# A sparse-attention and Fourier-mixing kernel: block sums and a mask moved to GpSimd, row statistics split between VectorE and ScalarE, one weight tile converted later

## The chip, the cores and the metric

The kernel runs on one core of a Trainium2 chip, in float32. The metric is the device time of one execution in microseconds. Engines are written as in the profile: PE (TensorE), DVE (VectorE), ACT (ScalarE), POOL (GpSimd), SP (SyncE, which here issues most of the transfers).

## The reference, cut to what matters

Four batches, eight heads, 768 tokens, 64 elements per head. Each token attends to its neighbours within 16 places and to one summary per block of 32 tokens (the maximum of the keys, the mean of the values). The result goes through a real Fourier mix over tokens and channels, a layer norm and a two-layer MLP.

```python
k_sum = k.reshape(B, H, nb, block, D).max(axis=3)
v_sum = v.reshape(B, H, nb, block, D).mean(axis=3)
...
a = softmax(concat([where(|i - j| < window, q k^T, -1e9), q k_sum^T + log(block)]))
attn_out = a @ concat([v, v_sum])
...
mixed = real(fft(fft(x, axis=1), axis=2))
u = x + mixed
mu = mean(u);  var = mean((u - mu) ** 2)
un = (u - mu) / sqrt(var + 1e-06)
return u + relu(un @ w_ch1) @ w_ch2
```

`w_ch1` (512 x 2048) and `w_ch2` (2048 x 512) arrive as 64-bit floats, which the kernel turns into 32-bit ones itself.

## The kernel before, in words

The program is one long sequence for the four batches, written with generators that are interleaved, so that the attention of batch b + 1 runs beside the MLP of batch b. Both MLP products are done by a Strassen-Winograd scheme with seven products instead of eight; its sums of operands and of results are additions on DVE, POOL and ACT, and its matmuls are the lines L1381 (hidden layer: hx, hy, hz), L1651 (o) and L1674 (ox, oy, oz).

**Batch 0's attention** (`first_attention`) goes head pair by head pair; its order on PE and DVE is written out by hand. Query and key tiles are transposed on PE (qk), scores (sc) go through an exponential on ACT into p, which DVE masks; p times values gives av, which DVE scales by the reciprocal of its last column into x. The summary values need sums over blocks of 32 rows: `add_blocks(gg)` (L606) halves a 96 x 2048 tile by five additions (1024, 512, 256, 128, 64 columns) into vbs, for heads 0 to 3 (gg = 0) and 4 to 7 (gg = 1); a matmul (vs, L767) spreads these.

**Batch 0's Fourier mix and norm** (`gen_fourier(0)`): after the folded token transform (t, f, y), the channel transform mx (L1297, L1299) is added to x on DVE for each of six tiles of 128 tokens, in two halves of three tiles. `bn_stats` and `bn_aggr` (L1306, L1307) give mean and variance of each row. For each half a chain of small operations on 128 x 3 elements (L1319 to L1331: sign, epsilon, a bit trick for the reciprocal root and three Newton steps) gives the factors; two tiles are then normalised on DVE (L1279) and one on ACT (L1276), into big. PE transposes big (unt, L1353), the copies (L1354) make u, and `_right_sums` makes the three Strassen sums of u on DVE (128 x 1536, 768, 768).

**Batch 1's attention** (`gen_attention(1)`) runs beside that: for each pair g of heads qk(1,g), sc(1,g), ss(1,g) (scores of the summaries, L811), av(1,g) (L829, L834), vs(1,g) (L817). ACT copies the qk tiles out of PSUM (L729, into kt and qt) and takes the exponentials (L800, L812). `add_later_blocks(1, gg)` (L642) makes batch 1's block sums from four 96 x 512 pieces: three additions and a `tensor_reduce` (L650) on DVE for batch 1, six additions on POOL for later batches. Tiles of batch 1's p are masked by `near` (L1048): for g = 0 on POOL, for g = 1 on DVE. All attention tiles share four PSUM banks (tag "attn"); the dense work has the other four.

**Weights** (`gen_weights`, plan at L1064): each tile of w_ch1 or w_ch2 is loaded as raw words (`load_raw`, issued by SP), converted by `exponents` and `convert` (in turn DVE L1096, ACT L1097, DVE L1109, ACT L1110, DVE L1112, DVE L1114 and a DVE multiplication), and for w_ch1 three Strassen sums follow. The finished tile is also stored to memory for the later batches (dw). An entry of the plan waits until the program has reached its stage: (1, 1), the second tile of w_ch1, waits for ("mx", 0).

**What sets the order.** The scheduler places instructions from the order of the program's text, with priorities. `tc.issue_after(marks[...])` keeps an instruction behind a marked one: the transposes of batch 0's first half stand behind the scores sc(1,0), those of the second half behind av(1,0) (L1347). On every engine instructions then run in the order of the program; SP's transfers too are issued in order.

Of the kernel before, what the change touches and what calls it, by code (L numbers as in the profile page):

```python
# [16 lines left out]
P = 128  # L17
# [471 lines left out]
def _main_program(ctx, tc, q, k, v, moe_w_ch1, moe_w_ch2, out):  # L489
# [116 lines left out]
    def add_blocks(gg):  # L606
        raw, vb = to_add[gg]
        n = BLOCK * D // 2
        while n > D:
            tt(raw[:, 0:n], raw[:, 0:n], raw[:, n:2 * n], ADD)  # L610
            n //= 2
        tt(vb, raw[:, 0:D], raw[:, D:2 * D], ADD)
# [29 lines left out]
    def add_later_blocks(b, gg):  # L642
        f = BLOCK // 4
        raw, vb = to_add[b, gg]
        add = gtt if b > 1 else tt
        add(raw[0], raw[0], raw[1], ADD)
        add(raw[2], raw[2], raw[3], ADD)
        add(raw[0], raw[0], raw[2], ADD)
        if b == 1:
            nc.vector.tensor_reduce(out=vb, in_=raw[0].rearrange("p (f d) -> p d f", d=D), op=ADD, axis=AX.X)  # L650
            return
        while f > 2:
            f //= 2
            gtt(raw[0][:, 0:f * D], raw[0][:, 0:f * D], raw[0][:, f * D:2 * f * D], ADD)
        gtt(vb, raw[0][:, 0:D], raw[0][:, D:2 * D], ADD)
# [149 lines left out]
    def sum_scores(b, g, p):  # L805
        km, qt = km_bufs[g % 2], nat[b, g]
        ps = abank([P, S2], f"ss_{b}_{g}")
        for h in range(2):
            for e in range(2):
                rows, r = slice(D * e, D * (e + 1)), 64 * (e ^ h) + 32 * h  # L810
                nc.tensor.matmul(ps[r:r + 32, :], km[rows, :], qt[rows, S2 * h:S2 * (h + 1)], start=True, stop=True)  # L811
        nc.scalar.activation(out=p, in_=ps, func=AF.Exp, scale=SC)  # L812
# [178 lines left out]
    def gen_attention(b):  # L991
# [13 lines left out]
        for g in range(NP + 1):  # L1005
# [42 lines left out]
            if b == 1 and g < 2:  # L1048
                for h in range(2):
                    with tc.issue_after(marks["u"]) if g else ExitStack():  # L1050
                        (tt if g else gtt)(held[0][:, h], held[0][:, h], near[:, h], ALU.mult)
# [93 lines left out]
    def gen_weights():  # L1145
        for f, j, stage in plan:
# [3 lines left out]
            while True:  # L1150

                with tc.issue_after(marks[stage]) if stage in marks else ExitStack():
                    done = next(steps, steps) is steps
                if done:
                    break
                yield
        for to, wv in stores:
# [66 lines left out]
    def gen_fourier(b):  # L1224
# [56 lines left out]
        for half in range(2):  # L1281
# [3 lines left out]
            if b == 0:  # L1285
                both = spool.tile([P, HT, 2], FP, tag="both", bufs=2, name=f"both_{half}")
            for i in range(HT):
# [4 lines left out]
                else:  # L1292
# [10 lines left out]
                    with tc.issue_after(marks["un", 0]) if t > HT else ExitStack():  # L1303
                        tt(xv, ps, xv, ADD)
                    bst = spool.tile([P, 6], FP, tag="bst", name=f"bst_{b}_{t}")
                    nc.vector.bn_stats(out=bst, in_=x[:, t, :])  # L1306
                    nc.vector.bn_aggr(out=both[:, i], in_=bst)  # L1307
# [23 lines left out]
            ins = nc.vector.tensor_tensor(out=z, in0=minus, in1=y, op=ALU.mult)  # L1331
            if b == 0:
# [9 lines left out]
        for t in range(NST):  # L1342
# [4 lines left out]
            with tc.issue_after(marks[("av", 1, 0) if half else ("sc", 1, 0)]) if b == 0 else ExitStack():  # L1347
# [10 lines left out]
            yield  # L1358
        _right_sums(tt, u.rearrange("p a k n -> p a (k n)"))
# [517 lines left out]
```

## Time and profile before

| | us |
|---|---|
| time of the kernel, median of 3 runs | 789.2 (786.87 to 791.82) |
| span of the profiled execution | 787.6 |
| PE busy | 771.0 (98%) |
| DVE busy | 536.3 (68%) |
| ACT busy | 241.8 (31%) |
| POOL busy | 74.6 (9%) |

The profiled execution is another than the three timed ones: its own time is known only as its span, from the first to the last instruction. The change touches the stretch from 25 to about 135 us. A row of the timeline has the start, the duration, the engine and line, the operation, what it writes and reads, how many instructions the row holds, and in brackets the idle time before it and what ended that. A row of the windows has the busy time of each engine in a stretch, the number of instructions in it, the mean granted TensorE clock and the share of DMA time. A row of the groups has busy time and the mean of one instruction in ns.

### The profile page before, as it was taken

The numbers are of one execution on the slowest core, as the hardware profiler recorded it, in microseconds if no ns is written. First come the engines' busy times: TensorE is split into PE (matmuls) and PEld (weight loads), VectorE is DVE, ScalarE is ACT, GpSimd is POOL, SyncE is SP. The second block draws the span as 40 slices with busy tenths as digits, with TensorE's granted clock in tenths as the row PEclk, the third lists the DMA queues.
The fourth block names the chain that finished last, engine by engine and source line by source line (L and its number), as shares of the span: only waits on it lengthen the run. The fifth ranks groups of instructions, "written<-read, shape, count | busy, mean of one in ns | idle before, by whom it ended". The sixth has DMA issues, their size and how long they took to land.

```text
span 787.6 us, 14943 instructions
## 1 busy us (share of the span) xinstructions
PE 771.0 (98%) x6076; PEld 582.2 (74%) x6076; DVE 536.3 (68%) x1121; ACT 241.8 (31%) x561; POOL 74.6 (9%) x99
## 2 busy tenths in 40 slices
PE   8999899999999999999999999999999999999997
PEld 5878455445579866688569876688659889889986
DVE  4899979697988647652577635463476987766762
ACT  3555557236535112100226112210126214204300
POOL 0000000000000020200120011300030004201500
PEclk9999999999999999999999999999999999999999
DMA  8999785796966369996344159830614044204001
GB/s 182 200 279 236 178 281 158 232 251 230 222 196 177 71 174 189 261 156 143 123 185 141 54 172 180 210 109 10 253 48 158 27 164 170 94 1 188 1 28 57
DMA packets 133933, 121.87 MB, mean 155 GB/s; under 512 B 94528, under 2 KB 115232, under 8 KB 133664
## 3 DMA queue, kind: packets, MB, share of 16 engines
q1 hardware_dynamic: 132736, 118.53, 54.8%
q0 software_dynamic: 576, 2.10, 0.7%
q8 instruction: 50, 0.82, 0.5%
q10 hardware_dynamic: 544, 0.20, 0.1%
q14 instruction: 27, 0.22, 0.1%
HBM read 97.22 MB, written 23.59 MB: 153 GB/s over the span
## 4 chain that ended last, share of the span: by engine, by line
PE 86%; DVE 7%; ACT 3%; DMA 2%; issue 1%; SPq 0%; DVEq 0%
PE ox L1674 18%; PE hx L1381 15%; PE oz L1674 9%; PE hz L1381 7%; PE oy L1674 4%; PE t L1554 4%; PE o L1651 4%; PE hy L1381 4%; PE y L1258 3%; PE f L1554 2%; PE mx L1217 2%; PE sc L793 2%; PE av L829 2%; DMA words<-in_v_dram 1%; PE av L834 1%; PE ss L811 1%
## 5 line engine op out<-in xcount | busy, mean ns | idle before, releaser
L1381 PE MATMUL hx<-u,w 128*128 128x384 f32 x384 | 140.4, 494 | 1.3 <-ACT h L1398 0.8
L1381 PEld LDWEIGHTS hx<-u,w 128*128 128x128 f32 x384 | 70.9, 190 | 53.5 <-ACT p L800 3.7
L1674 PE MATMUL oz<-w,s 128*128 128x256 f32 x336 | 81.7, 380 | 0.0
L1674 PE MATMUL ox<-w,s 128*128 128x256 f32 x336 | 80.1, 380 | 0.0
L1674 PE MATMUL ox<-w,h 128*128 128x256 f32 x336 | 79.6, 381 | 0.0
L1674 PEld LDWEIGHTS ox<-w,h 128*128 128x128 f32 x336 | 63.0, 190 | 10.7 <-issue 1.2
L571 DVE TENSOR_TENSOR x<-ox,x 128x256 f32<-128x256 f32 x84 | 35.5, 423 | 51.2 <-PE ox L1674 50.8
L1381 PE MATMUL hz<-u,w 128*128 128x384 f32 x192 | 70.3, 487 | 0.0
L1674 PEld LDWEIGHTS ox<-w,s 128*128 128x128 f32 x336 | 63.0, 190 | 9.3 <-DVE s L571 0.4
L1674 PEld LDWEIGHTS oz<-w,s 128*128 128x128 f32 x336 | 63.3, 190 | 8.9 <-DVE x L571 0.4
L1381 PEld LDWEIGHTS hz<-u,w 128*128 128x128 f32 x192 | 36.3, 190 | 25.0
L1392 ACT COPY h<-hx 128x384 f32<-128x384 f32 x24 | 11.5, 479 | 119.6 <-PE hx L1381 119.6
L1651 PE MATMUL o<-w,h 128*128 128x512 f32 x96 | 42.3, 595 | 0.7 <-DVE w L571 0.7
L1674 PE MATMUL oy<-w,h 128*128 128x256 f32 x168 | 40.7, 381 | 0.7 <-ACT h L1603 0.7
L1557 ACT COPY f<-t 128x192 f32<-128x192 f32 x52 | 15.8, 303 | 78.3 <-PE t L1554 78.1
L1533 POOL TENSOR_SCALAR h<-h 128x768 f32<-128x768 f32 x12 | 25.4, 2127 | 137.5 <-DVE h L1513 137.5
L574 POOL TENSOR_TENSOR vb<-vb 96x512 f32<-96x512 f32 (+2 forms) x20 | 20.9, 1050 | 182.4 <-DMA vb<-in_v_dram 116.2
L571 DVE TENSOR_TENSOR x<-oz,x 128x256 f32<-128x256 f32 x42 | 17.8, 423 | 26.7 <-PE oz L1674 26.4
L1674 PEld LDWEIGHTS oy<-w,h 128*128 128x128 f32 x168 | 31.5, 190 | 5.9 <-ACT h L1603 1.5
L1381 PE MATMUL hy<-u,w 128*128 128x384 f32 x96 | 35.2, 488 | 0.0
L1651 PEld LDWEIGHTS o<-w,h 128*128 128x128 f32 x96 | 18.0, 190 | 22.7 <-issue 20.7
L571 DVE TENSOR_TENSOR h<-hy,h 128x384 f32<-128x384 f32 x24 | 13.4, 556 | 26.3 <-PE hy L1381 26.1
(222 smaller groups left out, 1328.8 us busy)
## 6 DMA issues: line engine op xcount, KB each, us to landing
w<-dw SPq DMA_DIRECT2D x42, 896.0 KB, 5.9
words<-in_moe_w_ch_dram SPq DMA_DIRECT2D x32, 512.0 KB, 5.9
dw<-w SPq DMA_DIRECT2D x12, 896.0 KB, 7.6
vw<-in_v_dram SPq DMA_DIRECT2D x47, 192.0 KB, 6.2
out_dram<-x SPq DMA_DIRECT2D x23, 256.0 KB, 2.0
vb<-in_v_dram SPq DMA_DIRECT2D x24, 192.0 KB, 7.2
kn<-in_k_dram SPq DMA_DIRECT2D x9, 384.0 KB, 6.2
qn<-in_q_dram SPq DMA_DIRECT2D x9, 384.0 KB, 7.3
```

Source lines behind the costliest of these rows:

```text
L571: return nc.vector.tensor_tensor(out=out, in0=in0, in1=in1, op=op).ins
L574: return nc.gpsimd.tensor_tensor(out=out, in0=in0, in1=in1, op=op).ins
L793: ins = nc.tensor.matmul(ps[h][r:r + 64, i, :], kt[rows, o:o + 64], qt[rows, o:o + BLOCK], start=True, stop=True)
L829: nc.tensor.matmul(av[r][32 * j:32 * (j + 1), t, :], p[rows, h, i - NB2 * h, :], vw[rows, i, :], start=(t == 0), stop=False, skip_group_ch ...
L1217: nc.tensor.matmul(out, y[:, g], table, start=False, stop=True, skip_group_check=True)
L1258: nc.tensor.matmul(y, fgs[b][par][:, st, P * g:P * (g + 1)], fs[par][:, g % 2, st, :], start=(st == 0), stop=(st == n - 1))
L1381: ins = nc.tensor.matmul(ps, w[:, a, kk, :], u[:, r, kk, :], start=start and kk == 0, stop=stop and kk == 1, skip_group_check=True)
L1533: nc.gpsimd.tensor_scalar(out=t, in0=t, scalar1=0.0, scalar2=None, op0=ALU.max)
L1554: marks["two"] = nc.tensor.matmul(o, left(j, a, m), rhs(r, m), start=m in (1, 5), stop=m in (2, 3, 4, 5, 7), skip_group_check=True).ins
L1557: nc.scalar.copy(out={1: f[:, 0], 6: f[:, 1], 7: g}[m], in_=t)
L1651: nc.tensor.matmul(ps, h[:, n, hf, P * t:P * (t + 1)], wt[2, b, j][:, 2 * hf:2 * hf + 2, :], start=(n, hf) == (0, 0), stop=(n, hf) == (NC ...
L1674: nc.tensor.matmul(ps, left[a][:, n, :], wt[2, b, j][:, r, :], start=start and n == 0, stop=stop and n == NC - 1, skip_group_check=True)
```

## The change

Six things are done. (1) `add_blocks(1)`, the second set of batch 0's block sums, goes from DVE to POOL. (2) Batch 1's two sets of block sums go from DVE to POOL; the reduction becomes three smaller additions. (3) The mask of batch 1's pair g = 1 goes from DVE to POOL. (4) Batch 0's statistics: the addition of mx to x becomes a `scalar_tensor_tensor` that also gives the row sum; ACT squares (sum - 512 x) with a row sum of its own, so `bn_stats` and `bn_aggr` fall away, and with them one small operation per half; the scale 1/512^3 and the sign move into two of the small operations. (5) The transposes of batch 0's second half stand behind ss(1,0) and no longer behind av(1,0). (6) The second entry of the weight plan waits, after its first step, until the transposes of u have been written into the program.

```diff
     def add_blocks(gg):
...
+        add = gtt if gg else tt
         while n > D:
-            tt(raw[:, 0:n], raw[:, 0:n], raw[:, n:2 * n], ADD)
+            add(raw[:, 0:n], raw[:, 0:n], raw[:, n:2 * n], ADD)
             n //= 2
-        tt(vb, raw[:, 0:D], raw[:, D:2 * D], ADD)
+        add(vb, raw[:, 0:D], raw[:, D:2 * D], ADD)
...
     def add_later_blocks(b, gg):
-        add = gtt if b > 1 else tt
-        add(raw[0], raw[0], raw[1], ADD)
-        add(raw[2], raw[2], raw[3], ADD)
-        add(raw[0], raw[0], raw[2], ADD)
-        if b == 1:
-            nc.vector.tensor_reduce(out=vb, in_=raw[0].rearrange("p (f d) -> p d f", d=D), op=ADD, axis=AX.X)
-            return
+        gtt(raw[0], raw[0], raw[1], ADD)
+        gtt(raw[2], raw[2], raw[3], ADD)
+        gtt(raw[0], raw[0], raw[2], ADD)
         while f > 2:
...
     def sum_scores(b, g, p):
+        marks["ss", b, g] = ins.ins
...
     def gen_attention(b):
-                        (tt if g else gtt)(held[0][:, h], held[0][:, h], near[:, h], ALU.mult)
+                        gtt(held[0][:, h], held[0][:, h], near[:, h], ALU.mult)
...
     def gen_weights():
                 yield
+                if (f, j) == (1, 1) and stage != ("u", 0):
+                    stage = ("u", 0)
+                    while stage not in issued:
+                        yield
...
     def gen_fourier(b):
-                        tt(xv, ps, xv, ADD)
-                    bst = spool.tile([P, 6], FP, tag="bst", name=f"bst_{b}_{t}")
-                    nc.vector.bn_stats(out=bst, in_=x[:, t, :])
-                    nc.vector.bn_aggr(out=both[:, i], in_=bst)
+                        nc.vector.scalar_tensor_tensor(out=xv, in0=ps, scalar=1.0, in1=xv, op0=ALU.mult, op1=ADD,
+                                                       accum_out=minus[:, i:i + 1])
+                    nc.scalar.activation(out=un[:, t, :], in_=x[:, t, :], func=AF.Square, bias=minus[:, i:i + 1],
+                                         scale=-float(DM), accum_out=var[:, i:i + 1])
...
-            if b == 0:
-                nc.vector.tensor_scalar(out=minus, in0=both[:, :, 0], scalar1=-1.0, scalar2=None, op0=ALU.mult)
-                nc.vector.tensor_scalar(out=var, in0=both[:, :, 1], scalar1=1e-6, scalar2=None, op0=ADD)
-            else:
-                nc.vector.tensor_scalar(out=var, in0=var, scalar1=1.0 / DM, scalar2=1e-6, op0=ALU.mult, op1=ADD)
+            nc.vector.tensor_scalar(out=var, in0=var, scalar1=1.0 / DM ** (1 if b else 3), scalar2=1e-6, op0=ALU.mult, op1=ADD)
...
-            ins = nc.vector.tensor_tensor(out=z, in0=minus, in1=y, op=ALU.mult)
-            if b == 0:
+            if b:
+                tt(z, minus, y, ALU.mult)
+            else:
+                ins = nc.vector.scalar_tensor_tensor(out=z, in0=minus, scalar=-1.0 / DM, in1=y, op0=ALU.mult, op1=ALU.mult)
                 marks["mx", 0] = ins.ins
...
-            with tc.issue_after(marks[("av", 1, 0) if half else ("sc", 1, 0)]) if b == 0 else ExitStack():
+            with tc.issue_after(marks[("ss", 1, 0) if half else ("sc", 1, 0)]) if b == 0 else ExitStack():
...
+        if b == 0:
+            marks["u", 0] = marks["u"]
+        issued.add(("u", b))
         _right_sums(tt, u.rearrange("p a k n -> p a (k n)"))
```

The orders below show two places. In a name such as hx_3_1505 the first number is the tile and the last one an instance; lines are those of each kernel's own text, so the same statement may stand at L811 before and at L808 now.

The first place is PE where batch 0's second half is transposed. Before, the transposes unt_3 to unt_5 stand behind the last matmuls of av(1,0), directly ahead of ss(1,1):

```order
L834 MATMUL av_0_1_1086<-vs,p_0_954 128x2x65
L1353 MATMUL unt_3_1147<-ident,big_734 128x128 x4
L1353 MATMUL unt_4_1170<-ident,big_734 128x128 x4
L1353 MATMUL unt_5_1183<-ident,big_734 128x128 x4
L811 MATMUL ss_1_1160<-qt_1_831,km_83 32x384 x4
L726 MATMUL qk_2_0_1195<-ident,kn_2_725 128x128 x3
```

In the change they stand inside the scores sc(1,1) (the rows of unt_4 and unt_5 alternate four times):

```order
L790 MATMUL sc_1_1_1006<-qt_1_826,kt_81 64x32 x2
L790 MATMUL sc_1_0_1005<-qt_1_826,kt_81 64x32
L1351 MATMUL unt_3_1118<-ident,big_736 128x128 x4
L1351 MATMUL unt_4_1134<-ident,big_736 128x128
L1351 MATMUL unt_5_1140<-ident,big_736 128x128
```

So 12 transposes have moved ahead of 35 of the 48 pairs of score matmuls and of all of av(1,0).

The second place is ACT where batch 1's pair g = 3 is copied out of PSUM (kt_81 and qt_3 from qk_3). Before, the four copies of kt stand together behind the exponential of ss(1,2), and a weight conversion (words, w_0_1) stands ahead of the copies of qt:

```order
L812 ACTIVATE p_2_1466<-ss_2_1471 128x384
L729 COPY kt_81<-qk_3_0_1539 64x384 x2
L729 COPY kt_81<-qk_3_1_1545 64x384 x2
L1392 COPY h_0_1244<-hx_3_1505 128x384
L1389 ACTIVATE h_0_1244<-h_0_1244 128x384
L1398 COPY h_0_1244<-hx_3_1505 128x384
L1389 ACTIVATE h_0_1244<-h_0_1244 128x384 x2
L1411 ACTIVATE h_0_1244<-hx_2_1390 128x384
L1097 ACTIVATE words<-words,rebias 128x1024
L1110 ACTIVATE w_0_1_1366<-w_0_1_1366 128x1024
L1400 COPY h_0_1244<-hz_3_1507 128x384
L729 COPY qt_3_1538<-qk_3_0_1551 64x384 x2
```

In the change:

```order
L810 ACTIVATE p_2_1438<-ss_2_1443 128x384
L726 COPY kt_81<-qk_3_0_1511 64x384 x2
L726 COPY kt_81<-qk_3_1_1517 64x384
L1095 ACTIVATE words<-words,rebias 128x1024
L1108 ACTIVATE w_0_3_1346<-w_0_3_1346 128x1024
L1390 ACTIVATE h_0_1202<-h_0_1202 128x384
L1412 ACTIVATE h_0_1202<-hx_2_1363 128x384
L1390 ACTIVATE h_0_1202<-h_0_1202 128x384
L726 COPY kt_81<-qk_3_1_1517 64x384
L726 COPY qt_3_1510<-qk_3_0_1523 64x384 x2
L726 COPY qt_3_1510<-qk_3_1_1529 64x384 x2
L817 ACTIVATE vs<-vs_2_1536,half 128x64 x2
```

So the conversion of the fourth tile of w_ch1 (w_0_3) and three activations of the hidden layer now stand between the third and the fourth copy of kt.

The third place is PE after ss(1,2) in the change, where the transposes of qk(1,3), vs and av(1,2) come close together:

```order
L808 MATMUL ss_2_1443<-qt_2_1148,km_82 32x384 x4
L1382 MATMUL hx_2_1363<-u_802,w_0_2_1226 128x384 x2
L1382 MATMUL hz_2_1365<-u_802,w_0_2_1226 128x384 x2
L723 MATMUL qk_3_0_1511<-ident,kn_3_988 128x128 x3
L723 MATMUL qk_3_1_1517<-ident,kn_3_988 128x128 x3
L723 MATMUL qk_3_0_1523<-ident,qn_3_990 128x128 x3
L723 MATMUL qk_3_1_1529<-ident,qn_3_990 128x128 x3
L815 MATMUL vs_2_1536<-vbs_1_1185,sel 128x64
L1382 MATMUL hx_2_1363<-u_802,w_0_2_1226 128x384 x2
L827 MATMUL av_2_0_1587<-vw_84,p_2_1438 32x65 x17
```

Before, hidden-layer products of two tiles and six products of o (L1651) lay between the first of these transposes and av(1,2); now two matmuls of hx lie between vs(1,2) and it.

More of the change, by code (lines that the diff above doesn't have):

```diff
@@ L810, in sum_scores @@
                 rows, r = slice(D * e, D * (e + 1)), 64 * (e ^ h) + 32 * h
-                nc.tensor.matmul(ps[r:r + 32, :], km[rows, :], qt[rows, S2 * h:S2 * (h + 1)], start=True, stop=True)
+                ins = nc.tensor.matmul(ps[r:r + 32, :], km[rows, :], qt[rows, S2 * h:S2 * (h + 1)], start=True, stop=True)
+        marks["ss", b, g] = ins.ins
         nc.scalar.activation(out=p, in_=ps, func=AF.Exp, scale=SC)
@@ L1284, in gen_fourier @@
             minus, var = stat[:, 0], stat[:, 1]
-            if b == 0:
-                both = spool.tile([P, HT, 2], FP, tag="both", bufs=2, name=f"both_{half}")
             for i in range(HT):
@@ L1330, in gen_fourier @@
                 nc.vector.scalar_tensor_tensor(out=y, in0=z, scalar=1.5, in1=y, op0=ADD, op1=ALU.mult)
-            ins = nc.vector.tensor_tensor(out=z, in0=minus, in1=y, op=ALU.mult)
-            if b == 0:
+            if b:
+                tt(z, minus, y, ALU.mult)
+            else:
+                ins = nc.vector.scalar_tensor_tensor(out=z, in0=minus, scalar=-1.0 / DM, in1=y, op0=ALU.mult, op1=ALU.mult)
                 marks["mx", 0] = ins.ins
```

## The prediction

> **What bounds the kernel now.** I read the page first, then the list of what PE waits for, then the windows, then the timeline and the transfers where the waits lie.
>
> ```profile
> PE 771.0 (98%) x6076; PEld 582.2 (74%) x6076; DVE 536.3 (68%) x1121; ACT 241.8 (31%) x561; POOL 74.6 (9%) x99
> PE 86%; DVE 7%; ACT 3%; DMA 2%; issue 1%; SPq 0%; DVEq 0%
> ```
>
> PE is busy for 771.0 of 787.6 us. So all of its idle time is 16.6 us, and the change removes no matmul: work taken off DVE is worth only what PE waits for DVE. That list is short (line of the waiting matmul, what it waited for, us in total, times, longest):
>
> ```profile
> PE ss L811 <- issue: 2.5, 1, 2.5
> ...
> PE o L1651 <- DVE w L571: 0.7, 1, 0.7
> ...
> PE av L777 <- DVE p L571: 0.6, 1, 0.6
> ...
> PE ss L811 <- DVE km L700: 0.3, 1, 0.3
> ```
>
> The windows place it (busy us of each engine, then the granted clock and the DMA share):
>
> ```profile
> 60.00:80.00 20.00, 19.58 (x387) 16.80 (x386) 18.61 (x60) 10.71 (x22) 1.97 (x2) 1.00 1.19 243
> 80.00:100.00 20.00, 16.84 (x160) 9.15 (x158) 18.42 (x26) 11.09 (x21) 0.00 (x0) 0.91 0.70 162
> ...
> 120.00:140.00 20.00, 20.00 (x63) 10.92 (x62) 18.35 (x26) 12.43 (x24) 0.00 (x0) 1.00 0.70 178
> ```
>
> From 60 to 80 us DVE is the fuller helper (18.61 of 20), and the chain of work that ended last runs through its x, bst, norm and big lines there. Yet PE lost only 0.42 us in that window, since scores and av filled the time. From 120 to 140 us PE loses nothing at all. The one large loss is at 81 us, and it is no wait for DVE:
>
> ```profile
> 80.80 0.48 PE L811 MATMUL ss<-qt,km 64*32 64x384 f32 x1 [0.32 <-DVE km L700]
> 83.81 1.50 PE L811 MATMUL ss<-qt,km 64*32 64x384 f32 x7 [2.54 <-issue]
> ```
>
> PE stops in the middle of eight like matmuls. The transfers in these microseconds show why:
>
> ```profile
> DMA  9999999999999989777676655933221211100000
> ...
> q8 instruction: 1, 0.02, 3.7%
> ```
>
> This is 80 to 82 us: the data queue is full until 81.2, and the only instruction packet of the window (0.02 MB) starts when it drains. In the window from 76 to 80 us there is none, though the data queue runs at full share. I read it so: PE's next instructions queue behind the transfer issued last, qn at 75.52.
>
> ```profile
> 75.52 0.94 SPq L551 DMA_DIRECT2D qn<-in_q_dram  x1
> ```
>
> After the stop the granted clock is half for one stretch:
>
> ```profile
> 81.27:83.81 2.54, 0.00 (x1) 0.00 (x0) 2.54 (x4) 0.52 (x2) 0.00 (x0) 1.00 0.06 15
> 83.85:87.26 3.41, 3.41 (x13) 1.45 (x13) 3.41 (x5) 1.50 (x3) 0.00 (x0) 0.50 0.94 265
> ```
>
> 3.41 us at 0.50 cost up to 1.7 us more, so the stop is worth 2.54 + 1.7 = 4.2 us. [...]
>
> **The change part by part.**
>
> *Batch 0's second block sums to POOL.* DVE is freed of four additions, 2.72 us, and a small one:
>
> ```profile
> 29.38 2.72 DVE L571 TENSOR_TENSOR words<-words 96x1024 f32<-96x1024 f32 x4
> ```
>
> and the matmul that reads the sums stands at
>
> ```profile
> 34.11 0.63 PE L767 MATMUL vs<-vbs,sel 96*32 96x64 f32 x8
> ```
>
> The words are issued at 17.89 us and land 8.7 us later, at 26.6:
>
> ```profile
> L551 SPq DMA_DIRECT2D words<-in_v_dram x1: 493/493/493, 17.9 to 17.9; - x1
> ...
> DMA to landing us min/median/max: 8.7/8.7/8.7
> ```
>
> POOL's prices for such additions:
>
> ```profile
> L574 POOL TENSOR_TENSOR vb<-vb 96x512 f32<-96x512 f32 x12 | 15.8, 1324 | 181.8 <-DMA vb<-in_v_dram 116.2 <-ACT p L800 65.3
> ...
> L574 POOL TENSOR_TENSOR vb<-vb 96x256 f32<-96x256 f32 x4 | 2.9, 722 | 0.3
> ...
> L574 POOL TENSOR_TENSOR vb<-vb 96x128 f32<-96x128 f32 x4 | 2.2, 554 | 0.3
> ...
> L574 POOL TENSOR_TENSOR p<-p,near 128x384 f32<-128x384 f32 x2 | 2.0, 1006 | 28.6 <-ACT p L800 28.6
> ...
> L574 POOL TENSOR_TENSOR vbs<-vb 96x64 f32<-96x64 f32 x4 | 1.3, 315 | 0.3
> ```
>
> The 1024 columns are not shown; twice 1.32 is 2.65. The sum is 2.65 + 1.32 + 0.72 + 0.55 + 0.32 = 5.6 us, done at 32.2, 1.9 us ahead of the matmul that reads them. Cost 0; the cover is gone if the words land 1.9 us later. The gain is at most the 0.6 us that av L777 waited for p behind DVE's queue at 42 us.
>
> *Batch 1's block sums and the mask.* The reductions and the matmuls that read all such sums (duration least, median, most; first and last start):
>
> ```profile
> L817 PE MATMUL vs<-vbs,sel x24: 221/273/323, 74.3 to 520.6; 96*128 96x64 f32 x24
> ...
> L650 DVE TENSOR_REDUCE vbs<-vb x2: 1021/1022/1022, 61.2 to 123.5; 96x64 f32<-96x512 f32 x2
> ```
>
> DVE saves 1.02 us and three additions, about 0.68 each (what bst below takes over 512 columns), so 3.06 us twice, and two masks of some 0.55. POOL needs 3 x 1.32 + 0.72 + 0.55 + 0.32 = 5.6 us a set and 2.0 us for the masks. The first reduction ended at 62.2 and its matmul came at 74.3; the second at 124.5 and 130.04 (row below). 2.5 us more than now leaves over 9 us and 3 us. Cost 0.
>
> *Statistics.* What goes from DVE:
>
> ```profile
> L1306 DVE BATCH_NORM_STATS2 bst<-x 128x6 f32<-128x512 f32 x6 | 3.9, 679 | 0.0
> L1307 DVE BATCH_NORM_AGGREGATE both<-bst 128x2 f32<-128x6 f32 x6 | 1.0, 170 | 0.0
> ```
>
> That is 6 x 0.68 + 6 x 0.17: 5.1 us, and a small operation in each half. ACT gains six Squares, by the like operation of later batches 0.72 us each, 4.3 us, into the window where it was busy for 10.7 of 20:
>
> ```profile
> L1313 ACT ACTIVATE big<-x,stat 128x512 f32<-128x512 f32 x6 | 4.3, 717 | 0.1
> ```
>
> The addition with a row sum is not shown: from 0.68 us, as bst over the same 512 columns, to twice that if the sum takes a pass of its own, 4.1 us over six tiles. I take the first; at the other end the 3.5 us just below are gone and with them the gain.
>
> In the chain of the second half the last Square (0.72 and two handovers) stands where two bst and their aggregates stood (1.4 with overlap): little is gained there. But the half starts some 3.5 us sooner (one reduction, three bst, the aggregates). DVE was through with normalising when it took up the next weight tile, at 78.50; now that is near 75. PE begins the scores sc(1,1) at 74.66:
>
> ```profile
> 78.50 0.69 DVE L1096 TENSOR_SCALAR words<-words 128x1024 int32<-128x1024 int32 x1
> 74.66 1.58 PE L793 MATMUL sc<-qt,kt 64*64 64x32 f32 x91
> ```
>
> The transposes, moved ahead of 35 pairs of these scores, are reached by PE at about 75 too. Little or no wait: 0, at worst 1 us, and that would be spent ahead of the stop at 81 us.
>
> Together these three parts relieve PE of the waits for DVE in the list: the 0.3 at 80.80, perhaps the 0.6 of av. I take **-0.5** (from -0.9 to 0).
>
> *The stop at 81 us.* PE's matmuls up to it are the same ones in another order, so its instructions run out at the same count. kn and qn are issued by SP as before. PE reaches that count at best 0.3 us sooner and waits for the same transfer: I take **0**, with -4.2 as the other end if the order of the transfers has shifted enough. What is earlier in u is worth nothing then, as hidden products begin after the stop.
>
> *The later second weight tile.* DVE began its conversion at 78.50; now the transposes of u are written ahead of most of it. This pushes the conversions of the second, third and fourth tile back. Where it lands is ACT's queue at the copies of qk(1,3): between the third and fourth copy of kt stand a conversion and three activations. Their prices:
>
> ```profile
> L1097 ACT ACTIVATE words<-words,rebias 128x1024 int32<-128x1024 int32 x7 | 8.0, 1149 | 5.0 <-DVE words L1096 4.8
> L729 ACT COPY qt<-qk 64x384 f32<-64x384 f32 x13 | 6.7, 513 | 0.2
> L1110 ACT ACTIVATE w<-w 128x1024 f32<-128x1024 int32 x6 | 6.3, 1044 | 0.0
> ...
> L1389 ACT ACTIVATE h<-h 128x384 f32<-128x384 f32 x12 | 6.1, 522 | 5.4 <-DVE h L571 5.4
> ```
>
> av(1,2) needs two of the four attention banks, which these copies free. From the third copy of kt to the second copy of qt ACT has 0.51 + 1.15 + 1.04 + 3 x 0.52 + 0.51 + 2 x 0.51 = 5.8 us. PE has, in that time, about nine transposes, vs and two hx:
>
> ```profile
> 129.38 0.82 PE L726 MATMUL qk<-ident,qn 128*128 128x128 f32 x6
> 130.04 0.33 PE L817 MATMUL vs<-vbs,sel 96*128 96x64 f32 x2
> ```
>
> that is 1.2 + 0.3 + 0.8 = 2.3 us. So PE waits up to 3.5 us; nothing if ACT has run ahead by then. Before, some twenty dense products lay there and PE lost nothing. I take **+2.0**, nearer the full wait, since the orders of both engines show no other work in between. On PE all of the hidden layer is queued behind av(1,2), so this wait reaches the end undiminished. The 0.7 us that o waited for a converted w I count as gone, **-0.4** (from -0.7 to 0), because conversions of w_ch2 now have less in front of them on a lighter DVE.
>
> Sum: -0.5 + 0 + 2.0 - 0.4 = **+1.1**, a span of 788.7 against 787.6. The median of the runs is 1.6 above that profiled span, so the time is 790.3 us.
>
> **The rivals.**
>
> *The stop vanishes.* If in the new order the packet of instructions comes ahead of qn's transfer, 4.2 us fall away: 787.6 - 4.2 + 1.1 = 784.5, as a time 786.1; with no wait at av(1,2), 784. For it: the gap is a coincidence of a full queue and a count of instructions. Against: both stay where they were.
>
> *Slower: the wait at av(1,2) halves the clock.* The mechanism is ACT's queue: the copy that frees a bank stands behind a conversion, and the conversion behind DVE (idle of 4.8 us behind L1096 in the row above). From about 2.5 us of idleness the trace shows the clock halved for 3.41 us, 1.7 us more. With the full 3.5 us: 787.6 - 0.5 + 3.5 + 1.7 = 792.3, as a time 793.9, and up to 797 if the late tiles make hx wait as well. For it: DVE is at 18.35 of 20 in that window already. Against: DVE loses some 11 us of work ahead of it.
>
> *POOL holds up DVE.* POOL gets 18.8 us of additions (5.6 three times and 2.0). [...] In this trace, from 469.6 to 475.5 us with POOL adding all the time, DVE's masks took 1093 ns, while an addition of the same shape took 545:
>
> ```profile
> L571 DVE TENSOR_TENSOR p<-p,near 128x384 f32<-128x384 f32 x2 | 2.1, 1093 | 3.6 <-ACT p L800 3.6
> ...
> L571 DVE TENSOR_TENSOR h<-hx,h 128x384 f32<-128x384 f32 x1 | 0.5, 545 | 0.0
> ```
>
> So some operations double and others do not. If every operation beside POOL doubled, 18.8 us of POOL would cost DVE 9.4 us, as much as moved. Then the -0.5 and -0.4 are gone and the time is 787.6 + 2.0 + 1.6 = 791.2.
>
> *Nothing that can be measured changes:* av(1,2) finds ACT ahead, and the time stays at 788 to 789.
>
> **How the numbers follow.** The forecast, a slight loss with the stop in its place, 789 to 792.3: 0.42. The stop vanishes: 0.17. The halved clock at av(1,2): 0.17. POOL holds up DVE: 0.06. Nothing changes: 0.18. Predicted is the likeliest, 790.3 us. The range reaches from 785.0 to 795.5: the upper end takes in most of the slower rival, the lower end the 786.1 of the first and part of its further gain. A measurement of this kernel tells about 1% from no change, 7.9 us. Faster than 781.3 needs the whole stop to go and 4 us more of 16.6: 0.03. Slower than 797.1 needs the halved clock and a further wait: 0.06. Within: 0.91.
>
> **What would show it.** Right: POOL's vbs done near 32 us; no bst; un of the second half near 75 us; the gap with "issue" as its cause in ss L808 or the matmuls about it and a clock of 0.5 after it; between 115 and 135 us a wait of PE for ACT's kt or qt ahead of av. Wrong: no gap near 81 us, or DVE's rows longer beside POOL, or PE still without a loss from 100 to 140 us.

## The result, and the profile after

The change is slower by about 6 us: 794.15 us median (793.39 to 797.79, 6 runs) against 788.3 us (785.47 to 791.82), a ratio of 1.0075 with a 95% interval of 1.0051 to 1.0100. That is under the 1% named in the prediction and inside its range, but near the upper end.

The profiled execution has a span of 791.4 us. PE and DVE are as full as before, and POOL has gained 25 us, 6 more than the prediction's 18.8:

```profile
PE 773.2 (98%) x6076; PEld 586.4 (74%) x6076; DVE 538.6 (68%) x1098; ACT 247.4 (31%) x573; POOL 99.4 (13%) x118
```

5.1 us of statistics and some 10 us of sums and masks were taken off DVE, and its busy time has grown by 2.3 us: the rest of its operations got longer. That is the first thing to see. Already in batch 0's attention the eight operations `wide<-x` took 6.1 us in place of 4.2, and the masks of p 9.0 in place of 8.2, which gives back 2.7 of the 2.9 us that the second block sums had cost there. POOL's own work grew as well: batch 1's block sums took 8.2 and 8.5 us, not 5.6, and the mask of g = 1 took 3.1 us, not 2.0. The list of what PE waits for has two new heads, and a wait of hx behind them:

```profile
PE unt L1351 <- ACT big L1278: 3.5, 1, 3.5
PE av L827 <- ACT kt L726: 1.6, 1, 1.6
PE hx L1382 <- DVE h L571: 1.5, 2, 0.7
```

The "issue" wait in ss and the wait of o for w are gone from it. The windows place the two losses, in PE's busy time and in the granted clock behind it:

```profile
60.00:80.00 20.00, 16.54 (x212) 13.96 (x211) 15.85 (x51) 13.60 (x31) 3.31 (x4) 0.88 1.12 242
80.00:100.00 20.00, 19.59 (x235) 12.82 (x236) 18.74 (x23) 14.02 (x26) 6.76 (x5) 0.87 0.89 214
...
120.00:140.00 20.00, 17.15 (x136) 10.14 (x135) 18.14 (x25) 14.98 (x26) 0.00 (x0) 0.91 1.06 302
```

**The first loss, at 73.6 us.** PE's timeline:

```profile
72.96 0.65 PE L790 MATMUL sc<-qt,kt 64*64 64x32 f32 x26
77.08 2.82 PE L1351 MATMUL unt<-ident,big 128*128 128x128 f32 x12 [3.46 <-ACT big L1278]
79.83 2.14 PE L790 MATMUL sc<-qt,kt 64*64 64x32 f32 x70
```

After 26 score matmuls PE reaches the transposes that were moved there and stands for 3.46 us; the 70 matmuls that used to fill this time stand behind. The clock then is half for 6.8 us:

```profile
73.60:77.10 3.50, 0.04 (x2) 0.03 (x1) 3.17 (x12) 1.13 (x3) 0.92 (x1) 0.71 1.10 280
77.10:80.50 3.40, 3.40 (x37) 3.07 (x40) 2.77 (x5) 1.97 (x6) 0.00 (x0) 0.50 0.92 234
80.50:83.90 3.40, 3.40 (x154) 3.16 (x152) 3.40 (x4) 2.67 (x4) 1.21 (x2) 0.50 0.02 7
83.90:87.30 3.40, 3.40 (x28) 2.12 (x26) 3.40 (x4) 1.21 (x3) 1.80 (x1) 0.80 1.10 168
```

At 0.50 and at 0.80 of full speed these stretches cost, as an estimate from the granted clock, up to 3.4 x 0.5 + 3.4 x 0.5 + 3.4 x 0.2 = 4.1 us more; twelve transposes took 2.82 us at 0.50 here and 1.53 us at 70.36 us, where the clock was 1.00. Together 7.6 us, against 5.0 before (0.42 + 0.32 + 2.54 of waits and 1.7 of clock).

Why is big late? DVE's rows of the second half's chain, and POOL's row of the same moment:

```profile
72.01 0.17 DVE L1318 TENSOR_SCALAR stat<-stat 128x3 f32<-128x3 f32 x1 [0.89 <-ACT big L1306]
...
72.62 0.96 DVE L1324 SCALAR_TENSOR_TENSOR norm<-norm 128x3 f32<-128x3 f32 x1
73.62 0.92 DVE L571 TENSOR_TENSOR norm<-norm,stat 128x3 f32<-128x3 f32 x1
74.57 0.16 DVE L1326 SCALAR_TENSOR_TENSOR norm<-norm 128x3 f32<-128x3 f32 x1
```

```profile
72.57 1.95 POOL L574 TENSOR_TENSOR p<-p,near 128x384 f32<-128x384 f32 x2 [11.13 <-ACT p L797]
```

The chain begins 0.89 us late, behind the last Square on ACT, and two operations on three columns, which elsewhere take 0.16 us, take 0.96 and 0.92 while POOL multiplies the mask in two instructions of 1.00 and 0.99 us. The mask ran on POOL at this time before too (at 72.65), but DVE then stood at other work (x from mx, with an operand in PSUM, and bst, with one operand), which was not held up: 0.68 us each, the mean of their groups. The same is seen 15 us earlier beside POOL's new block sums:

```profile
54.37 3.62 POOL L574 TENSOR_TENSOR vb<-vb,vb 96x512 f32<-96x512 f32 x2 [0.28 <-DMA vb<-in_v_dram]
58.06 2.99 POOL L574 TENSOR_TENSOR vb<-vb 96x256 f32<-96x256 f32 x2
```

```profile
52.86 1.77 DVE L1107 TENSOR_SCALAR w<-words 128x1024 int32<-128x1024 int32 x1
54.89 1.96 DVE L1110 SCALAR_TENSOR_TENSOR words<-words 128x1024 int32<-128x1024 int32 x1 [0.26 <-ACT words L1095]
56.77 2.29 DVE L1112 SCALAR_TENSOR_TENSOR w<-words,w 128x1024 f32<-128x1024 uint32 x1
59.10 1.63 DVE L571 TENSOR_TENSOR w<-w,words 128x1024 f32<-128x1024 f32 x1
```

Before, L1110 and L1112 took (their lines there are L1112 and L1114; groups of the first 130 us, us in total and mean ns):

```profile
L1112 DVE SCALAR_TENSOR_TENSOR words<-words 128x1024 int32<-128x1024 int32 x6 | 7.4, 1230 | 3.6 <-ACT words L1097 3.6
L1114 DVE SCALAR_TENSOR_TENSOR w<-words,w 128x1024 f32<-128x1024 uint32 x5 | 6.1, 1223 | 0.0
```

So the last three steps of one tile's conversion lost 0.7 + 1.1 + 0.4 = 2.2 us (the third against 1.22 too), and the chain 0.8 + 0.8 = 1.6 us. L1107, which reads one operand from SBUF and took 0.69 us before, grew by 1.1 us beside POOL's first addition (52.80 to 54.09), but DVE had to wait for ACT's words behind it in any case. By what means POOL lengthened these operations, no row shows. Each of the two short operations grew by most of the POOL instruction beside it (0.80 of 1.00 us and 0.76 of 0.99), the three long ones by less (0.7, 1.1 and 0.4 us, beside instructions of 1.3 to 2.1 us).

**The second loss, at 121 us.** It stands where the prediction put it. PE's rows, then ACT's:

```profile
122.11 1.56 PE L1382 MATMUL hx<-u,w 128*128 128x384 f32 x4 [0.75 <-DVE h L571]
125.27 0.75 PE L827 MATMUL av<-vw,p 64*32 64x65 f32 x34 [1.60 <-ACT kt L726]
126.32 1.51 PE L827 MATMUL av<-vw,p 64*32 64x65 f32 x56 [0.30 <-ACT qt L726]
```

```profile
119.80 1.59 ACT L726 COPY kt<-qk 64x384 f32<-64x384 f32 x3 [1.80 <-PE qk L723]
121.42 1.15 ACT L1095 ACTIVATE words<-words,rebias 128x1024 int32<-128x1024 int32 x1
122.47 1.04 ACT L1108 ACTIVATE w<-w 128x1024 f32<-128x1024 int32 x1
...
124.72 0.49 ACT L726 COPY kt<-qk 64x384 f32<-64x384 f32 x1
```

The fourth copy of kt, which frees the bank that av(1,2) needs, comes 3.3 us after the third, with a conversion and three activations between them. PE loses 0.75 + 1.60 + 0.30 = 2.65 us, of which 1.90 at av for ACT's copies and 0.75 at hx for DVE's h, and then runs below the full clock (0.91 over the window). The 0.7 us that o waited for w is saved.

### The profile page after: what moved, and what is told of

The parts are those of the page before. It is cut to its first block, busy times and chain, and to the rows that moved or that the text cites. A ratio compares the mean times of both kernels' runs of the same rounds, so it can differ in the third digit from the quotient of the medians.

```text
span 791.4 us, 14961 instructions
## 1 busy us (share of the span) xinstructions
PE 773.2 (98%) x6076; PEld 586.4 (74%) x6076; DVE 538.6 (68%) x1098; ACT 247.4 (31%) x573; POOL 99.4 (13%) x118
## 4 chain that ended last, share of the span: by engine, by line
PE 86%; DVE 7%; ACT 4%; SPq 1%; issue 1%; DMA 0%; POOL 0%; DVEq 0%; ACTq 0%; POOLq 0%
PE ox L1675 17%; PE hx L1382 14%; PE oz L1675 9%; PE hz L1382 7%; PE o L1652 5%; PE oy L1675 4%; PE t L1555 4%; PE hy L1382 3%; PE y L1260 3%; PE f L1555 2%; PE sc L790 2%; PE mx L1219 2%; PE av L827 2%; SPq L551 1%; PE av L832 1%; PE g L1555 1%
## 5 line engine op out<-in xcount | busy, mean ns | idle before, releaser
L574 POOL TENSOR_TENSOR vb<-vb 96x512 f32<-96x512 f32 (+2 forms) x24 | 25.3, 1058 | 182.2 <-DMA vb<-in_v_dram 115.5
```

What stands on the lines that cost most here:

```text
L574: return nc.gpsimd.tensor_tensor(out=out, in0=in0, in1=in1, op=op).ins
```

## The experiments

Two theories stood against each other. One: the loss is made by the order, in two waits of PE, at the transposes that were moved ahead of the scores and at av(1,2) behind the later conversion. The other: it is made by what was moved to POOL and ACT, whatever the order. A third came up on the way: what limits the stretch from 73 to 83 us is the order of ACT's queue, in which big stands among the exponentials. Where an expectation names theories by letters, its own sentences give what each makes of that run; what follows is told here by their content. Each kernel was timed beside the kernel before, whose median in these series was 788.5 to 788.9 us. Diffs are against the changed kernel unless another is named.

**1. The mark of the second half's transposes put back.**

```
-            with tc.issue_after(marks[("ss", 1, 0) if half else ("sc", 1, 0)]) if b == 0 else ExitStack():
+            with tc.issue_after(marks[("av", 1, 0) if half else ("sc", 1, 0)]) if b == 0 else ExitStack():
```

> The change with one part undone: the transposes of the second half stand behind av(1,0) again. Theory A (the transposes put ahead of the scores are what PE waits for): the wait of 3.46 us for big and the two stretches of half clock after it (77 to 84 us) go, 3.46 + about 3.4 us, while the stop in ss near 81 us comes back with its 4.2 us if it is a matter of the transfer ahead of the instructions: 794.15 - 6.9 + 4.2 = 791.4 us, with unt following av without a wait. Theory B (the statistics on ScalarE made big late for any order): PE waits for big at the later place as well, 793 to 794 us.

Measured: 791.15 us, ratio 1.0033 (1.0015 to 1.0052). About half of the loss is gone, and with it the wait for big. But the old stop in ss did not come back. In its place PE waits 2.98 us ahead of av(1,0), with no releaser named:

```profile
75.12 0.31 PE L790 MATMUL sc<-qt,kt 64*64 64x32 f32 x5 [0.26 <-issue]
78.42 2.00 PE L827 MATMUL av<-vw,p 64*32 64x65 f32 x96 [2.98 <-issue]
```

```profile
76.64 0.82 ACT L1278 ACTIVATE big<-x,norm 128x512 f32<-128x512 f32 x1 [2.38 <-DVE norm L1330]
77.36 0.56 ACT L1352 COPY u<-unt 128x512 f32<-128x512 f32 x1
77.83 0.49 ACT L810 ACTIVATE p<-ss 128x384 f32<-128x384 f32 x1
```

ACT stands 2.38 us for the norm chain with big at the head of its queue; the exponential of ss(1,0) and the scaling vs, which av(1,0) reads, stand behind it, though PE was done with the matmuls of ss at 73.0 us and with those of vs at 73.4. In the kernel before, this exponential (74.43) and vs (74.82) stand ahead of big (77.58) in ACT's order. So the size came out as the theory of the order has it, but that is luck in part: the old stop was to come back, and in its place came a new one, made by ACT, which took the exponential (77.83) after big (76.64), in the order of the program.

**2. The second weight tile converted when it was before.**

```
-                if (f, j) == (1, 1) and stage != ("u", 0):
-                    stage = ("u", 0)
-                    while stage not in issued:
-                        yield
```

> The change with one part undone: the second weight tile is converted as before, without the wait for the transposes of u. Theory A (that wait put a conversion between the copies of kt and so made av(1,2) wait): the 0.75 + 1.60 + 0.30 us of waiting between 121 and 127 us and the lower clock behind it (about 1.7 us) go, the 0.7 us of o for w come back: 794.15 - 4.35 + 0.7 = 790.5 us; the wait of unt for big stays at 3 to 4 us. Theory B (the wait at av(1,2) comes from the lighter or later hidden work and not from the weight tile): 794 us, and PE still loses over 2 us between 115 and 130 us.

Measured: 790.65 us, 1.0029 (1.0013 to 1.0045). The four copies of kt stand together again, and PE loses nothing from 120 to 140 us, at full clock:

```profile
120.00:140.00 20.00, 19.98 (x66) 10.95 (x64) 16.86 (x23) 13.94 (x25) 0.00 (x0) 1.00 0.76 189
```

The wait for big is still there, 3.2 us. This is the second loss by itself, worth 3.6 us (1.0075 - 1.0029 of 788.7).

**3. Both put back**, the two edits above together.

> The change with two parts undone: mark and weight tile as before, so that only the sums and the mask on GpSimd and the statistics are left. Theory A: both losses go and the stop near 81 us is back; 794.15 - 6.9 + 4.2 - 3.65 = 787.8 us, equal to before within 1 us. Theory B (GpSimd or the statistics cost time by themselves): 790 us or more.

Measured: 788.87 us, 0.9999 (0.9989 to 1.0010). The two parts of the order carry the whole loss: 3.3 and 3.6 us alone, 6.0 together. With sums, masks and statistics on POOL and ACT there is then no gain. But the kernel is not free of losses by the order: the old stop in ss, which the expectation had back, is not there, and the new one of experiment 1 is (this trace is of the slowest of the 13 executions, 792.28 us):

```profile
81.03 2.01 PE L827 MATMUL av<-vw,p 64*32 64x65 f32 x96 [3.00 <-issue]
```

What the rest is worth without that stop is asked in experiment 7.

**4. The first mask on POOL marked to come after the second half's norm.**

```
-                    with tc.issue_after(marks["u"]) if g else ExitStack():
+                    with tc.issue_after(marks["u"]) if g else tc.issue_after(marks["un", 1]):
```

> The change with the mask of batch 1's first pair on GpSimd held back until the second half of batch 0 is normalised. Theory A (two small operations of the norm chain on VectorE, 0.96 and 0.92 us in place of 0.16, stood still while GpSimd ran the mask's two operations): both rows are 0.16 to 0.2 us again, big is ready 1.6 us sooner, PE's wait for it is 1.9 us instead of 3.46, and the clock perhaps stays full: 789 to 792.6 us. Theory B (their length has another cause): the rows stay near 0.9 us and the time at 794 us.

Measured: 793.47 us, 1.0060 (1.0043 to 1.0076). It decides nothing: the mask ran at 73.23 us all the same, and the two short operations again took 0.96 and 0.92 us. Such a mark orders the program; it makes POOL, which has nothing else to do, wait for nothing.

**5. The first mask on DVE, behind the norm chain.**

```
-                    with tc.issue_after(marks["u"]) if g else ExitStack():
-                        gtt(held[0][:, h], held[0][:, h], near[:, h], ALU.mult)
+                    with tc.issue_after(marks["u"] if g else marks["un", 1]):
+                        (gtt if g else tt)(held[0][:, h], held[0][:, h], near[:, h], ALU.mult)
```

> The change with the mask of batch 1's first pair on VectorE, behind the second half of big. Theory A (GpSimd's mask held up two small operations of the norm chain): both rows 0.16 us, PE's wait for big 1.9 us instead of 3.46, with less half clock behind it: 789.2 to 792.5 us. Theory B (no such hold-up): rows of 0.9 us and 794 us; VectorE's own 1.1 us for the mask would then make it 794 to 795.

Measured: 790.54 us, 1.0046 (1.0023 to 1.0068), some 2.3 us less than the change by the ratios and 3.6 by the medians. The intervals of the two ratios overlap, and the twelve times lie in two groups, seven from 787.9 to 790.7 us and five from 792.3 to 796.3, so the price in time is not settled. What the run settles is the cause of the long rows, in a trace of the faster group (789.75 us). The two short operations of the chain, and PE at the transposes behind it:

```profile
73.28 0.16 DVE L1324 SCALAR_TENSOR_TENSOR norm<-norm 128x3 f32<-128x3 f32 x1
73.48 0.16 DVE L571 TENSOR_TENSOR norm<-norm,stat 128x3 f32<-128x3 f32 x1
```

```profile
76.18 1.53 PE L1351 MATMUL unt<-ident,big 128*128 128x128 f32 x12 [1.82 <-ACT big L1278]
```

```profile
80.00:100.00 20.00, 18.14 (x211) 11.15 (x194) 19.56 (x23) 11.50 (x23) 10.21 (x6) 1.00 0.85 225
```

The wait fell from 3.46 to 1.82 us, by the 1.6 us that the chain had lost, and in this execution the clock stayed full. Part of it goes again: ss(1,1) now waits 1.32 us for DVE's km. So the first loss is a wait made by the order, and 1.6 us of its length came from the mask beside the chain: the two theories meet there.

**6. Tile early (2) and mask on DVE (5) together.**

> The change with the weight tile converted as before and the first pair's mask on VectorE; the transposes stay ahead of the scores and the loads are as in the change. Theory A (the two losses are independent: 3.6 us of the mask on GpSimd and 3.5 us of the weight tile): 794.15 - 3.6 - 3.5 = 787.0 us, 1 to 2 us under the kernel before. Theory B (the late loads were not what made the earlier version with these two edits slow): 790 to 791.6 us.

Measured: 788.43 us, 1.0003 (0.9976 to 1.0030). Two small repairs other than putting the mark back bring the changed kernel to the time before, and no further. By the ratios their single gains are 3.6 and 2.3 us and together 5.7, so they add up; by the medians, as in the expectation, the sum would be 1.4 us better, which lies inside the interval. The trace (an execution of 790.67 us) also shows that a full clock does not follow from the shorter wait. The wait is as in experiment 5, and the clock halves behind it all the same:

```profile
77.04 1.95 PE L1347 MATMUL unt<-ident,big 128*128 128x128 f32 x12 [1.92 <-ACT big L1274]
```

```profile
80.40:83.80 3.40, 3.40 (x81) 2.55 (x74) 3.40 (x2) 1.77 (x3) 1.93 (x2) 0.50 0.76 194
```

**7. Both put back (3), and the second half's odd big tile on DVE**, so that ACT's queue holds none of that half's normalising:

```
-                if t % 2 and not (b == 0 and t == NST - 1):
+                if t % 2 and not (b == 0 and half):
```

> The change with mark and weight tile as before and, in the second half of batch 0, the tile of big that ScalarE normalised put on VectorE. Theory C (the stop of 3.0 us ahead of av(1,0) in the version with both parts back is ScalarE's queue: big, which waits for the norm chain, stands ahead of the exponential of ss(1,0) and of vs): ScalarE takes ss and vs at about 75 us, av(1,0) starts without that gap, and the instruction packet near 80 us decides next, with a stop of 1 to 2.5 us in ss(1,1): 785.5 to 788 us. Theory D (that gap is a lack of instructions): it stays at about 3 us where it was and the time is 789 to 790 us, as big comes 0.5 us later.

Measured: 788.15 us, 0.9997 (0.9978 to 1.0015). The wait ahead of av(1,0) is gone, since the exponential and vs are no longer behind big:

```profile
74.56 0.55 ACT L810 ACTIVATE p<-ss 128x384 f32<-128x384 f32 x1
74.94 0.56 ACT L817 ACTIVATE vs<-vs,half 128x64 f32<-128x64 f32 x2
```

```profile
76.08 1.24 PE L827 MATMUL av<-vw,p 64*32 64x65 f32 x96
...
81.16 0.51 PE L808 MATMUL ss<-qt,km 64*32 64x384 f32 x1 [1.50 <-ACT p L797]
82.72 0.84 PE L808 MATMUL ss<-qt,km 64*32 64x384 f32 x7 [1.05 <-issue]
```

That confirms the place of the wait in ACT's queue. A wait of 0.82 us is left at the end of sc(1,1). But the time won is given back 5 us later: PE comes early to ss(1,1), waits 1.50 us for an exponential, and then stands between the first and the second ss matmul, as in the kernel before.

**8. The kernel before, with the loads of (1,3) issued one step later.** This asks what the old stop in ss is.

```
+            if (b, g) == (1, 2):
+                load(1, 3)
...
-            if n3 and not (b == 1 and n3 > (2, 0)):
+            if n3 and not (b == 1 and n3 > (2, 0)) and n3 != (1, 3):
```

> The kernel before with one thing moved: the loads of batch 1's last head pair (kn_3, qn_3) are issued one pair later. Theory A (PE stops at 81 us because its next instructions stand behind these transfers): the stop of 2.54 us and the half clock go, 788.9 - 4.2 = 784.7 us, and the instruction packet lands within 2 us of the last one. Theory B (the stop hangs on the count of instructions alone): the stop stays and the time is 788 to 789 us.

Measured: 787.05 us, 0.9984 (0.9969 to 0.9999), the fastest of all kernels here, though its interval ends just short of 1. The packet of instructions now comes between 79 and 80 us, where before it came after 81, and the stop shrinks from 2.54 to 0.72 us:

```profile
q8 instruction: 1, 0.02, 7.2%
```

```profile
82.34 0.84 PE L811 MATMUL ss<-qt,km 64*32 64x384 f32 x7 [0.72 <-issue]
```

The gain is 1.6 us and not the 4.2 that the stop was priced at: a wait of 0.8 us for km now stands ahead of it, and the clock halves all the same (0.91 from 80 to 100 us). So the transfers ahead of the packet bear on the stop; what the 0.72 us that are left wait for is open.

**9 to 12. Combinations**, made to gain from both sides.

Both put back (3) with the late loads (8):

> The change with mark and weight tile as before, and the loads of kn_3 and qn_3 one pair later. Theory A: its stop of 3.0 us near 80 us and some 3 us of half clock go: 788.9 - 4.5 to 6 = 783 to 784.5 us, and what the lighter VectorE is worth shows against the kernel before with late loads. Theory B: 788.5 to 789 us.

Measured: 790.78 us, 1.0030 (1.0013 to 1.0047). PE waits 2.54 us ahead of av(1,0), ACT's queue again, and 2.1 us at hx for DVE's h.

Tile early and mask on DVE (6) with the late loads (8):

> The change with the weight tile converted as before, the first pair's mask on VectorE and the loads of kn_3 and qn_3 one pair later; the transposes stay ahead of the scores. Theory A: of the 3.2 us that PE waits for big some 1.6 stay, no clock is lost, and no stop follows: 790.65 - 1.6 - 1.5 - 1 = 786.5 us. Theory B (PE's wait for big does not depend on the mask): 790 us. If it is slower than the version with the mark put back and late loads, the mark costs time for every supply of instructions.

Measured: 791.58 us, 1.0032 (1.0016 to 1.0048). The wait for big is 1.4 us, but hx waits 3.6 us for h. Beside 6 (1.0003) the later loads bring no gain here and perhaps a loss, as the two intervals overlap; why h is late then was not followed further.

Both put back, big on DVE (7), and the mask on DVE (5):

> As the version with mark and weight tile back and all of the second half's big on VectorE, and with the first pair's mask on VectorE as well. Theory C with the hold-up by GpSimd: the norm chain ends 1.6 us sooner, PE does not wait for big, and only the stop for instructions near 80 us is left: 785.5 to 787.5 us. If the stop for instructions is unavoidable with the loads as they are, it grows by what PE comes sooner, and the time equals that version's within 0.5 us.

Measured: 788.81 us, 1.0005 (0.9986 to 1.0023). PE waits 2.95 us ahead of av(1,0) again. The cause is the mask itself: on DVE it stands behind the norm chain, big and two steps of a conversion, and av(1,0), which reads it, starts about when the first of its two operations is done. ACT had finished vs by 75.8:

```profile
77.86 1.02 DVE L571 TENSOR_TENSOR p<-p,near 128x384 f32<-128x384 f32 x2
```

```profile
78.51 1.75 PE L827 MATMUL av<-vw,p 64*32 64x65 f32 x96 [2.95 <-issue]
```

The same with the late loads (8):

> The version with mark and weight tile back, big's second half and the first pair's mask on VectorE, and the loads of kn_3 and qn_3 one pair later. Theory A (the stop near 81 us is instructions behind these transfers): no stop over 0.8 us, no half clock between 75 and 95 us, 783 to 785 us. Theory B (late loads move the waits to the second and third weight tile, as hidden products waiting for VectorE's h showed in the earlier late-load versions): 787 to 790 us.

Measured: 789.16 us, 1.0013 (0.9997 to 1.0028), with the same gap, 2.8 us. None of the combinations beats the kernel before; 8 alone does, by less than a quarter of a per cent.

## Why the prediction was right, and where it was wrong

**The time** is in the range and within 1%. The sum was +1.1 us; the runs show 5.9, so the size was not forecast, only the direction. That the miss is no larger is luck: a loss was left out (at the transposes), and the stop that was to stay fell away, and the two errors partly cancel.

**The signs.** Of the signs that the prediction named for being wrong two came: no gap near 81 us, and DVE's rows longer beside POOL. Of those for being right there came the sums on POOL (done at 29.6), the missing bst and the wait ahead of av; big of the second half was done at 77.0 and not near 75.

**What bounds the kernel** was read rightly. Some 15 us taken off DVE brought nothing (0.9999 in experiment 3, 0.9997 in 7). That fits a PE that had waited for DVE for less than 2 us, but does not prove it, as each of these kernels also has a stop of its own, and DVE's busy time did not fall.

**Batch 0's second sums** cost nothing, as said. They took 6.1 us on POOL (5.6 in the prediction) and ended at 29.6, and the matmul that reads them came at 32.97. The cover was larger than reckoned because the words landed earlier, by 23.4 us; DVE paid 2.7 us beside them, which PE did not wait for.

**The relief of -0.5** is there in the list of waits (km's 0.3 is gone, p's 0.6 is 0.3), but no run shows it in the time. It took DVE's remaining operations at their old durations, and beside POOL they grew (`wide<-x` from 4.2 to 6.1 us, the masks of p from 8.2 to 9.0). The rival "POOL holds up DVE" was this growth, at a chance of 0.06. It was priced as a loss of the relief alone; here it made a wait longer, by 1.6 us (3.46 us with it, 1.82 without it, experiment 5), and by a mask that was on POOL before the change too. The two rows by which the prediction judged the rival differ in their operands: the mask of 1093 ns reads both from SBUF, the addition of 545 ns reads hx from PSUM.

**The step that failed** is "Little or no wait: 0, at worst 1 us" for the transposes that were moved. It reckoned that the second half would be through near 75 us, 3.5 us sooner than before. PE reached the transposes at 73.6 and big let it go on at 77.08. This execution ran 1.6 us ahead of the one before (sc at 68.83 against 70.44), so on the earlier scale PE came at 75.2, as said, and was let go at 78.7. The chain of small operations began at 74.92 in the kernel before:

```profile
74.92 0.17 DVE L1319 TENSOR_SCALAR stat<-both 128x3 f32<-128x3 f32 x1
```

In the change it began at 72.01, which is 73.6 on the earlier scale: 1.3 us sooner and not 3.5. So 2.2 us were lost ahead of the chain, and 1.6 in it, beside the mask; that is the miss at big. Ahead of the chain DVE's rows show three delays: 2.2 us on the conversion beside POOL's block sums, 1.67 in which DVE waited for a Square that stood behind copies of kt in ACT's queue, and 0.89 for the last Square. They add up to 4.8 us where 2.2 are missing, and no run shows how much of each reached the chain. PE sets a limit as well, which the prediction's 3.5 us left out: its last mx, which the last addition to x reads, ended at 68.9 us, and that addition began at 70.34. ACT's six Squares were counted by their busy time in a window in which ACT had room; that their place in its queue is on the chain's path was left out of the sum, but for the last one.

**The stop at 81 us** was forecast to stay. The reading of its cause is borne out by experiment 8: with less data ahead of it the instruction packet came earlier, between 79 and 80 us, and the stop shrank from 2.54 to 0.72 us, though not to nothing. That it stays in the changed kernel was wrong. The prediction took PE to reach the same count of instructions at the same time; with 3.46 us lost and the clock halved just ahead of it, PE came to ss(1,1) at 85.09 us, while the packet came between 81 and 82 as before: on that reading, too late to run out. In the other runs, too, the stop stands only where PE comes to ss(1,1) by 81.2 us (before, 7 and 8), and nowhere that it comes later.

**The wait at av(1,2), +2.0**, was right in place, mechanism and size: 1.90 us at av for the copies of kt and qt. The 0.75 us at hx, where PE waited for DVE's h, were not in the sum. The lowered clock behind it belongs to its price (experiment 2 gained 3.6 us). The saving of 0.4 at o was 0.7.

**The slower rival** gave 793.9 us for 794.15 measured, but not by the way it was argued: it had the whole loss at av(1,2), and it came in two places, of which the larger in waiting time was the one forecast at nothing.

## What to carry to other kernels

In these traces work on GpSimd was paid by VectorE operations beside it that read only SBUF, mostly those with two operands there, and a chain of very short ones on the path paid most for its size (0.16 us became 0.96, a conversion step of 1.22 us became 2.29): look at what stands on VectorE at that time before moving anything. Where a stage is split over two engines that each take their instructions in the order of the program, as ACT did in experiment 1, count the handovers and what stands at the head of the second queue; the loss appears on a third engine, at times with no cause but "issue" (2.98 us ahead of av(1,0) there). And work that is put ahead of TensorE's filler has to be ready with a margin, since after 3.46 us of idleness there the clock was 0.50 for 6.8 us and 0.80 for 3.4 us, by the estimate above up to 4.1 us more.

## What the runs showed of the hardware

- Two operations of 0.16 us on VectorE took 0.96 and 0.92 us beside a GpSimd multiply of about 1 us each, and 0.16 without it. Additions with an operand in PSUM, and the statistics with a single operand, were not lengthened at the same place (0.68 us each); a conversion step with a single operand in SBUF was, from 0.69 to 1.77 us, beside a GpSimd addition of 1.29 us. No row shows by what means.
- The length of one idle time does not settle whether TensorE's clock halves. It halved after 2.54 us for 3.4 us (the kernel before), and after 3.46 us for 6.8 us (the change); it stayed full after 1.82 us (experiment 5) and after 1.50 + 1.05 us (7), and halved after 1.92 us (6) and after 0.8 + 0.72 us (8). What else counts is open.
- Instructions came in 50 packets of 0.82 MB in all (queue q8), about 16 KB each. One of them came between 79 and 80 us, and not after 81, when the loads of one head pair were issued a step later, and a stop in the middle of eight like matmuls went from 2.54 to 0.72 us. That TensorE's instructions wait behind data transfers issued earlier is the reading that fits; no row shows such a wait by name.
